# Split weights read from a second, displaced load: six vector operations in place of eight, and sums of three more attention slots on VectorE

## The chip, the cores and the metric

The kernel runs on one core of a Trainium2 chip. The metric is device time in microseconds (us) of one execution; the time of a version is the median over its runs.

## The reference

Attention with capped scores, then a mixing block ("spectral mix") on its result. B = 8 batches, H = 12 heads, S = 448 tokens, D = 64:

```python
scores = scale * np.matmul(q, k.transpose(0, 1, 3, 2))
scores = cap * np.tanh(scores / cap)
attn = np.exp(scores - max); attn = attn / sum(attn)
x = (attn @ v) laid out as [B, 448, 768]
theta = x @ w_theta
zr, zi = x * cos(theta), x * sin(theta)
u = x + w_tok_r @ zr + w_tok_i @ zi
out = u + np.maximum(u @ w_ch, 0.0)
```

The weights w_theta, w_tok_r, w_tok_i and w_ch come as 64-bit floating point numbers, the rest as float32. The kernel returns the transposed output; the host transposes it.

## The kernel before

**Work.** Attention is cut into 24 slots, three to a batch. A slot s is four heads, that is two pairs of heads (k = 2s and 2s+1); a pair's q and k are two tiles of 128 x 448 (two heads of 64 rows). Slots 0 to 3 hold attention alone. From slot LEAD = 4 on, the attention of slot s is interleaved with the mixing block of an earlier batch, a third of a batch per slot: the first third computes theta, its sine and cosine and the products (T, y, d, sc, r, f), the second mixes tokens (M), the third multiplies by w_ch (C).

**Order.** Everything stands in an order written by hand, one script of words for each kind of slot (PARTS, FRONT, OTHER at the end of the listing), and each engine runs its instructions in that order. S0 to S3 are the score matmuls (scores, L282) of a slot, t0 to t3 the tanh (L313) and e0 to e3 the exp (L326) on ScalarE (ACT); V0, W, Vr multiply by v (L376, L370), Ra and Rb sum the rows (L403); I inverts the sums and spreads them by four DMAs (L421), N multiplies (L428). The sums of slot s and its products with v, except the first ones, run in slot s+1. v loads v (L236, by the ACT queue from slot 1 on), q0, q1 load the next slot's q and k (L232, SyncE's queue, SP). The score banks in PSUM exist once, so S2 waits until t1 has read S1's scores, and v has one buffer.

**Row sums.** For s < DIRECT (direct, before 7) TensorE sums the tiles of exp themselves: 32 instructions. Else VectorE (DVE) first adds a pair's three tiles and the rest in six operations (words a0a, a0b, a1a, a1b; L346, L349, L350) and TensorE sums the result with 8.

**Weights.** A block of weights (th0 to th5: 768 words a row; tk0 to tk6: 448; ch0a to ch5b: 384) is loaded as 64-bit words and split into a high part hi and a low part lo that TensorE multiplies separately. Class Split does it: load (L135) by the queue of SP (">"), ACT ("%") or POOL ("@"); a scale on DVE ("#", L142) or on ACT ("*"); then in three parts a shift (L169), sign (L170), the AND that leaves the exponent (L153), the low word times it (L154), hi rounded (L159, or by ACT L157 for ch from 2 on), the rest (L160) and lo (L161). Which step stands in which slot is said by WEIGHTS (words w0 to w3) for th and tk and by the words that begin with ":" in slots 5 and 6 for ch. The raw words lie in large buffers, of which four (STAGES) serve th and tk; q, k and x lie in small ones.

**Queues.** DMAs issued by SP and ACT take eight counters in turn (DMAHW0 to DMAHW7 in the order below); an issue waits until the DMA before it on its counter has landed. Those of POOL have eight of their own (DMASW0 to 7).

Ahead of the branch on the size of cap the kernel loads q0, k0, th0 and th1, and TensorE runs some small matmuls (fill, L124); behind it follow q1, k1 and the scripts.

## Time and profile before

| what | value |
|---|---|
| median of 3 runs | 895.66 us (894.44 to 895.67) |
| profiled execution, its span from first to last instruction | 892.5 us |
| TensorE (PE) busy | 878.9 us, 98% |
| VectorE (DVE) busy | 658.8 us, 74% |
| ScalarE (ACT) busy | 572.9 us, 64% |
| GpSimd (POOL) busy | 92.5 us, 10% |
| chain that ended last, by engine | PE 88%, DVE 5%, ACT 2%, DMA 2%, issue 2% |
| start of slots 1, 4, 5, 6, 7 (first S0) | 22.4, 68.8, 103.0, 145.2, 184.5 us |

The profiled execution's span lies 3.2 us under the median, which includes what stands around the program. The chain of waits is followed back from the last instruction; where it lies on one engine for long, that engine sets the time there.

### The profile page before, as it was taken

To read this page: it belongs to the slowest core of one execution; us is meant where nothing else is said; L and a number is where in the kernel's file an instruction comes from. 1 tells how busy PE (TensorE), PEld (TensorE's weight loads), DVE (VectorE), ACT (ScalarE), POOL (GpSimd) and SP (SyncE) were. 2 spreads that over 40 slices of the span, in tenths; PEclk is the share of its full clock that TensorE was granted. 3 is DMA by queue.
4 is the path that set the end of the run, shared out by engine and by line. 5 is a ranking of instruction groups with operands and counts; after the bars stand their busy time and mean duration, and the time that the engine had idled before them with its cause. 6 is when DMAs were issued, how large, how long until landed. Compare 5 with 4: busy or idle time off the path is not lost.

```text
span 892.5 us, 13316 instructions
## 1 busy us (share of the span) xinstructions
PE 878.9 (98%) x4896; PEld 643.2 (72%) x4896; DVE 658.8 (74%) x1095; ACT 572.9 (64%) x652; POOL 92.5 (10%) x189
## 2 busy tenths in 40 slices
PE   8999999999999999999999999999999999999996
PEld 4325675768768678687686686776876866879995
DVE  6899779978876598675985679855987659855831
ACT  6887965658955598547975489564994459824420
POOL 0000110101300022000310012100130003100300
PEclk9999999999999999999999999999999999999998
DMA  7562464432413325122342233233151322311501
GB/s 268 191 208 73 109 172 123 151 115 72 127 50 114 94 65 152 58 88 73 107 121 68 73 108 108 80 94 114 53 145 51 104 84 80 97 42 28 139 12 55
DMA packets 50668, 90.70 MB, mean 102 GB/s; under 512 B 10913, under 2 KB 42273, under 8 KB 50593
## 3 DMA queue, kind: packets, MB, share of 16 engines
q1 hardware_dynamic: 40752, 64.62, 24.1%
q0 software_dynamic: 6384, 14.20, 5.9%
q10 hardware_dynamic: 3456, 10.95, 4.0%
q8 instruction: 40, 0.66, 0.3%
q14 instruction: 36, 0.29, 0.1%
...
## 4 chain that ended last, share of the span: by engine, by line
PE 88%; DVE 5%; ACT 2%; DMA 2%; issue 2%; SPq 1%; ACTq 0%; DVEq 0%
PE s L282 13%; PE a L376 12%; PE th L445 7%; PE th L446 7%; PE ch L445 7%; PE th L447 7%; PE ch L447 6%; PE ch L446 6%; PE mx L533 6%; PE mx L535 6%; PE mx L534 6%; PE r L403 4%; PE a L370 2%; ACT p L313 1%; DMA k<-in_qk 1%
## 5 line engine op out<-in xcount | busy, mean ns | idle before, releaser
L313 ACT ACTIVATE p<-s,qscale 128x1792 f32<-128x1792 f32 (+1 forms) x58 | 97.9, 1689 | 96.5 <-PE s L282 86.8
L506 POOL DMA_DIRECT2D t<-g_row x152 | 75.9, 506 | 536.6 <-DVE x_row L428 225.3
L533 PE MATMUL mx<-wtk_h,zh 128*128 128x448 f32 x336 | 124.4, 370 | 0.0
L535 PE MATMUL mx<-wtk_h,zl 128*128 128x448 f32 x336 | 123.4, 367 | 0.8 <-DVE zl L523 0.7
L534 PE MATMUL mx<-wtk_l,zh 128*128 128x448 f32 x336 | 122.9, 366 | 0.0
L326 ACT ACTIVATE p<-p,cap_sb 128x1792 f32<-128x1792 f32 (+1 forms) x77 | 119.9, 1558 | 2.5 <-PE a L376 1.9
L445 PE MATMUL ch<-us,wch_h 128*128 128x448 f32 x288 | 106.8, 371 | 0.4 <-DVE x L549 0.4
L445 PE MATMUL th<-xs,wth_h 128*128 128x448 f32 x288 | 106.9, 371 | 0.0
L446 PE MATMUL th<-xs,wth_h 128*128 128x448 f32 x288 | 105.5, 366 | 0.0
L447 PE MATMUL th<-xs,wth_l 128*128 128x448 f32 x288 | 105.4, 366 | 0.0
L447 PE MATMUL ch<-us,wch_l 128*128 128x448 f32 x288 | 105.3, 366 | 0.0
L446 PE MATMUL ch<-us,wch_h 128*128 128x448 f32 x288 | 105.3, 366 | 0.0
L376 PE MATMUL a<-p,v 128*64 128x448 f32 x496 | 102.6, 545 | 0.0
L376 PEld LDWEIGHTS a<-p,v 128*64 128x64 f32 x496 | 33.1, 136 | 57.1 <-issue 53.9
L533 PEld LDWEIGHTS mx<-wtk_h,zh 128*128 128x128 f32 x336 | 63.1, 188 | 10.7 <-issue 3.1
L535 PEld LDWEIGHTS mx<-wtk_h,zl 128*128 128x128 f32 x336 | 63.1, 188 | 7.6 <-DVE zl L523 2.3
L534 PEld LDWEIGHTS mx<-wtk_l,zh 128*128 128x128 f32 x336 | 63.1, 188 | 5.2
L523 DVE TENSOR_TENSOR zl<-t,zh 128x512 fp32r<-128x512 f32 x84 | 50.4, 616 | 16.5 <-ACT zh L516 15.2
L549 DVE SCALAR_TENSOR_TENSOR x<-ch,x 128x448 f32<-128x448 f32 x43 | 26.6, 621 | 48.7 <-PE ch L447 48.7
L445 PEld LDWEIGHTS ch<-us,wch_h 128*128 128x128 f32 x288 | 54.1, 188 | 10.0 <-issue 3.8
L445 PEld LDWEIGHTS th<-xs,wth_h 128*128 128x128 f32 x288 | 54.1, 188 | 9.4 <-issue 3.7
L282 PE MATMUL s<-q,k 64*128 64x448 f32 (+1 forms) x264 | 55.8, 559 | 2.5 <-DMA k<-in_qk 1.3
...
## 6 DMA issues: line engine op xcount, KB each, us to landing
v<-in_v ACTq DMA_DIRECT2D x23, 448.0 KB, 3.5
...
```

What stands on the lines that cost most here:

```text
L282: nc.tensor.matmul(out[h][:, :S], kk[rows], qq[rows], start=m == 0, stop=m == len(products) - 1)
L313: nc.scalar.activation(pp, t[:, :m, :, :S], AF.Tanh, scale=qscale)
L326: nc.scalar.activation(pp, pp, AF.Exp, scale=cap_sb)
L376: nc.tensor.matmul(acc_of["a", s, i][h * D : (h + 1) * D, :S], vt[s][:, 6 * i + 3 * h + c, :], U[s, (i, c)][:, h, :], start=first and c == ...
L445: nc.tensor.matmul(acc[:, :S], wh[:, j, ms], t[:, 0, :], start=j == 0, stop=False)
L446: nc.tensor.matmul(acc[:, :S], wh[:, j, ms], t[:, 1, :], start=False, stop=False)
L447: nc.tensor.matmul(acc[:, :S], wl[:, j, ms], t[:, 0, :], start=False, stop=j == NJ - 1)
L506: queue.dma_start(t[32 * m : 32 * m + 32, d * S : (d + 1) * S], f[32 * d : 32 * d + 32, m * S : (m + 1) * S])
L523: nc.vector.tensor_tensor(zl, tokens(b, j)[:, c0:c1], zh.bitcast(F32), op=ALU.subtract)
L533: nc.tensor.matmul(acc[:, :S], zh, wtk_h[:, c, :], start=c == 0, stop=False)
L534: nc.tensor.matmul(acc[:, :S], zh, wtk_l[:, c, :], start=False, stop=False)
L535: nc.tensor.matmul(acc[:, :S], zl, wtk_h[:, c, :], start=False, stop=c == NC2 - 1)
```

## The change

- DIRECT goes from 7 to 4: slots 4, 5 and 6 get their sums from tiles that DVE has added; the words a0a to a1b are put into the scripts of slots 4 to 6.
- Each weight block is loaded twice: once as before, and once two bytes displaced (the 16-bit view from its second element), so that a 32-bit word of the second load holds the middle bits of the 64-bit one. The split becomes six vector operations: scale, shift with AND (one instruction), sign, AND, an AND on the middle word, and one that makes lo.
- hi is no longer rounded by a cast with a subtraction behind it: it is cut by the AND. For th0 to th4 and tk0 to tk4 it is written by a DMA of the POOL queue from a working tile ("carried"), for th5, tk5, tk6 and all halves of ch by a copy on ACT. The scale of ch2b and ch3b moves to ACT.
- A th block takes two large buffers. The order of loads and splits in WEIGHTS is another: three th blocks are split in slot 0, and tk0 and tk1 are loaded behind th3.
- q1 and k1 are loaded ahead of the branch, th1 behind it; of the small buffers two move from one pool to the other.
- In slots 5 and 6 the words for ch stand in another order, and I of slot 5 earlier.

The diff, cut to its core (of the scripts, the first half of slot 5's):

```diff
-DIRECT = 7
+DIRECT = 4
...
-    w_tok = w_tok.bitcast(I32).rearrange("c p (n two) -> c p n two", two=2)
-    w_theta, w_ch = (w.bitcast(I32).rearrange("m p j (n two) -> m p j n two", two=2) for w in (w_theta, w_ch))
+    w_tok = [w_tok.bitcast(t) for t in (I32, U16)]
+    w_theta, w_ch = ([w.rearrange("m p j n -> m p (j n)").bitcast(t) for t in (I32, U16)] for w in (w_theta, w_ch))
...
-    small = Rooms(const, wk, "x", S, 2, 20)
+    small = Rooms(const, wk, "x", S, 4, 18)
...
-        def __init__(self, room, src, hi, lo, act=False):
-            self.room, self.src, self.hi, self.lo, self.act = room, src, hi, lo, act
+        def __init__(self, name, room, src, hi, lo, carried=False):
+            self.name, self.room, self.src, self.hi, self.lo, self.carried = name, room, src, hi, lo, carried
 
         def load(self, queue):
-            self.g, raw, self.t = self.room()
-            queue.dma_start(raw.bitcast(I32), self.src)
-            self.hw, self.lw = raw[..., 1], raw[..., 0]
+            self.gs, raw, self.mid, self.n = self.room()
+            queue.dma_start(raw.bitcast(I32), self.src[0])
+            queue.dma_start(self.mid.bitcast(U16)[:, : 4 * self.n - 1], self.src[1][:, 1:])
+            self.hw, self.low = raw[:, 1::2], raw[:, ::2]
+
+        def rows(self, t):
+            return t.rearrange("p (j n) -> p j n", n=P) if len(self.hi.shape) == 3 else t
...
         def part(self, stage):
+            hw, mw, lw = (self.rows(t) for t in (self.hw, self.mid[:, ::2], self.low))
             if stage == 0:
-                return self.first()
-            t, hi, lo, hw, lw = self.words, self.hi, self.lo, self.hw, self.lw
-            if stage == 1:
-                nc.vector.tensor_scalar(hw.bitcast(I32), t.bitcast(I32), -(2**23), None, op0=ALU.bitwise_and)
-                nc.vector.scalar_tensor_tensor(lw, lw.bitcast(U32), 2.0**-52, hw, op0=ALU.mult, op1=ALU.mult)
+                if self.carried:
+                    lw = self.rows(wk.tile([P, self.n], F32, tag="ps", name=f"t_{self.name}", bufs=2))
+                ti = lw.bitcast(I32)
+                nc.vector.tensor_scalar(ti, hw.bitcast(I32), 3, 0x7FFFF000, op0=ALU.logical_shift_left, op1=ALU.bitwise_and)
+                nc.vector.scalar_tensor_tensor(ti, hw.bitcast(I32), -(2**31), ti, op0=ALU.bitwise_and, op1=ALU.bitwise_or)
+                if self.carried:
+                    nc.gpsimd.dma_start(self.hi.bitcast(I32), ti)
+                nc.vector.tensor_scalar(hw.bitcast(I32), ti, -(2**23), None, op0=ALU.bitwise_and)
+            elif stage == 1:
+                nc.vector.tensor_scalar(mw.bitcast(I32), mw.bitcast(I32), 0x01FFFFFF, None, op0=ALU.bitwise_and)
             else:
-                if self.act:
-                    nc.scalar.copy(hi, t)
-                else:
-                    nc.vector.tensor_copy(hi, t)
-                nc.vector.tensor_tensor(t, t, hi.bitcast(F32), op=ALU.subtract)
-                nc.vector.tensor_tensor(lo, t, lw, op=ALU.add)
-                large.give(self.g)
-
-        def first(self):
-            t, hw = self.t, self.hw
-            if t is None:
-                t = wk.tile([P, DM], F32, tag="ps", name=f"t_{self.g.name if hasattr(self.g, 'name') else len(fills)}", bufs=2).rearrange("p (j n) -> p j n", j=NJ)
-            self.words, ti = t, t.bitcast(I32)
-            nc.vector.tensor_scalar(ti, hw.bitcast(I32), 3, None, op0=ALU.logical_shift_left)
-            nc.vector.scalar_tensor_tensor(ti, hw.bitcast(I32), -(2**31), ti, op0=ALU.bitwise_and, op1=ALU.bitwise_or)
+                if not self.carried:
+                    nc.scalar.copy(self.hi, lw)
+                nc.vector.scalar_tensor_tensor(self.lo, mw.bitcast(U32), 2.0**-36, hw, op0=ALU.mult, op1=ALU.mult)
+                for g in self.gs:
+                    large.give(g)
 
...
-            g = large.take([P, 4 * S], F32, f"{name}_raw", STAGES)
-            return g, g[:, : 2 * DM].rearrange("p (j n two) -> p j n two", j=NJ, two=2), None
+            gs = [large.take([P, 4 * S], F32, f"{name}_{part}", STAGES) for part in ("raw", "mid")]
+            return gs, gs[0][:, : 2 * DM], gs[1][:, : 2 * DM], DM
...
-            steps["th", str(m)] = Split(room_block(f"swh{m}"), w_theta[m], wth_h[:, :, ms], wth_l[:, :, ms])
+            steps["th", str(m)] = Split(f"th{m}", room_block(f"swh{m}"), [w[m] for w in w_theta], wth_h[:, :, ms], wth_l[:, :, ms], m < 5)
             for i, half in enumerate("ab"):
                 js = slice(i * NJ // 2, (i + 1) * NJ // 2)
-                steps["ch", f"{m}{half}"] = Split(room_half(f"swc{m}{half}", 1 - 2 * i), w_ch[m][:, js], wch_h[:, js, ms], wch_l[:, js, ms], m > 1)
+                src = [w[m][:, i * w.shape[2] // 2 : (i + 1) * w.shape[2] // 2] for w in w_ch]
+                steps["ch", f"{m}{half}"] = Split(f"ch{m}{half}", room_half(f"swc{m}{half}", 1 - 2 * i), src, wch_h[:, js, ms], wch_l[:, js, ms])
-            steps["tk", str(c)] = Split(room_tok(f"swk{c}"), w_tok[c], wtk_h[:, c], wtk_l[:, c])
+            steps["tk", str(c)] = Split(f"tk{c}", room_tok(f"swk{c}"), [w[c] for w in w_tok], wtk_h[:, c], wtk_l[:, c], c < 5)
...
-        (0, 0): ">th2 >tk0", (0, 1): "#th0 th0 >th3", (0, 2): "#th1 th1 >tk1", (0, 3): "#tk0 tk0 >th4",
-        (1, 0): "#th2 th2 >tk2", (1, 2): "#th3 th3 >tk3", (2, 0): "#tk1 tk1", (2, 1): "#tk2 tk2 >tk4", (2, 2): "#th4 th4 >th5", (2, 3): "",
-        (3, 0): "#tk3 tk3", (3, 1): "#tk4 tk4 >tk5", (4, 2): "#th5 th5 >tk6",
-        (4, 0): "#tk5 tk5", (4, 1): "#tk6 tk6", (4, 2): "#th5 th5 >tk6", (4, 3): "",
-        (6, 0): "#ch3a ch3a >ch4a #ch3b ch3b >ch4b", (6, 1): "#ch4a ch4a >ch5a #ch4b ch4b >ch5b", (6, 2): "#ch5a ch5a #ch5b ch5b",
+        (0, 0): ">th1", (0, 1): "#th0 th0 >th2", (0, 2): "#th1 th1 >th3", (0, 3): "#th2 th2 >tk0 >tk1",
+        (1, 0): "#th3 th3 >th4", (1, 2): "#tk0 tk0 >tk2", (1, 3): "#tk1 tk1 >tk3", (2, 0): "#th4 th4", (2, 2): "#tk2 tk2 >tk4", (2, 3): "#tk3 tk3 >tk5",
+        (3, 0): "#tk4 tk4 >tk6", (4, 2): "#tk5 tk5", (4, 0): "#tk6 tk6 >th5", (4, 1): "#th5 th5",
...
-        LEAD + 1: "S0 t0 Vr V0 Ra h0a l0a h0b l0b W h1a Rb :%ch0a cV0 cV1 :@ch0b sc2 Pa1 S1 Pb1 q0 t1 v M0a l1a r4 h1b M0b r5 l1b f4 f5 D2 e0 h2a M1a l2a m0 :#ch0a :0ch0a e1 M1b h2b l2b :1ch0a"
-        " S2 t2 M2a h3a :2ch0a :@ch1a l3a M2b h3b l3b I m1 M3a h4a l4a :#ch0b :0ch0b M3b h4b l4b :1ch0b e2 m2 S3 q1 t3 M4a h5a l5a :2ch0b :@ch1b :#ch1a :0ch1a m3 M4b"
+        LEAD + 1: "S0 t0 Vr V0 Ra h0a l0a h0b l0b W h1a Rb :%ch0a cV0 cV1 :@ch0b sc2 Pa1 S1 Pb1 q0 t1 v M0a l1a r4 h1b M0b r5 l1b I f4 f5 D2 e0 h2a M1a l2a m0 :#ch0a :ch0a :@ch1a e1 M1b h2b l2b"
+        " S2 t2 M2a h3a l3a a0a M2b h3b l3b :#ch0b :0ch0b m1 M3a h4a l4a :1ch0b :2ch0b :@ch1b M3b h4b l4b a0b e2 m2 S3 q1 t3 M4a h5a l5a :#ch1a :0ch1a m3 M4b"
...
-        for part in range(2):
-            load_raw(1, part)
...
-    for part in range(2):
-        load_raw(0, part)
-    for step in (("th", "0"), ("th", "1")):
-        steps[step].load(nc.sync)
+    for k in range(2):
+        for part in range(2):
+            load_raw(k, part)
+    steps["th", "0"].load(nc.sync)
```

The queue of SP from th2's load on, before (swh_raw, swk_raw and g_row are buffers of th and tk; in_wth is w_theta, in_wtok the token weights):

```order
L135 DMA swh_raw<-in_wth 128x1536 [waits DMAHW4_49]
L135 DMA swk_raw<-in_wtok 128x896 [waits DMAHW5_49]
L135 DMA g_row<-in_wth 128x1536 [waits DMAHW6_49,DVE_49]
L135 DMA g_row<-in_wtok 128x896 [waits DMAHW7_49,DVE_49]
L135 DMA swh_raw<-in_wth 128x1536 [waits DMAHW5_49,DMAHW0_49,DVE_49]
L232 DMA q_244<-in_qk 128x448 [waits DMAHW1_49]
L232 DMA k_246<-in_qk 128x448 [waits DMAHW2_49]
```

and with the change:

```order
L136 DMA g_row<-in_wth 128x1536 [waits DMAHW6_49,DVE_49]
L137 DMA g_row<-in_wth 128x3071 [waits DMAHW7_49]
L136 DMA swh_raw<-in_wth 128x1536 [waits DMAHW4_49,DMAHW0_49,DVE_49]
L137 DMA swh_mid<-in_wth 128x3071 [waits DMAHW5_49,DMAHW1_49]
L136 DMA g_row<-in_wtok 128x896 [waits DMAHW6_49,DMAHW2_49,DVE_49]
L137 DMA g_row<-in_wtok 128x1791 [waits DMAHW3_49]
L136 DMA g_row<-in_wtok 128x896 [waits DMAHW7_49]
L137 DMA g_row<-in_wtok 128x1791
L230 DMA q_246<-in_qk 128x448
L230 DMA k_248<-in_qk 128x448
```

The loads of th2 and th3 stand twice, tk0 and tk1 behind both, and the q and k of slot 2 behind those.

ACT at the beginning of slot 1, before:

```order
L313 ACTIVATE p_0_242<-s_0_237,qscale 128x1792 [waits PE_49]
L381 COPY x_0_258<-a_0_198 128x448
L236 DMA v_260<-in_v 128x896 [waits DMAHW7_49,DMAHW6_49,PE_49]
L326 ACTIVATE p_0_242<-p_0_242,cap_sb 128x1792 [waits Activation_49]
L313 ACTIVATE p_1_281<-s_1_274,qscale 128x1792 [waits PE_49]
```

and with the change:

```order
L311 ACTIVATE p_0_244<-s_0_239,qscale 128x1792 [waits PE_49]
L379 COPY x_0_260<-a_0_196 128x448
L234 DMA v_262<-in_v 128x896 [waits DMAHW7_49,DMAHW4_49,PE_49]
L324 ACTIVATE p_0_244<-p_0_244,cap_sb 128x1792 [waits Activation_49]
L311 ACTIVATE p_1_284<-s_1_277,qscale 128x1792 [waits PE_49]
```

The load of v waits for another counter: DMAHW4 in place of DMAHW6. Its last user ahead is tk1's first load (before: a th load).

ACT in slot 5, before (zh is the high part of z, L157 and L168 write hi of w_ch):

```order
L516 CAST zh_933<-g_row 128x384 [waits DVE_49,PE_49]
L326 ACTIVATE p_0_906<-p_0_906,cap_sb 128x1792
L516 CAST zh_933<-t_1_878 128x512 [waits DMAHW0_49,DMAHW1_49,DMASW7_49,DMAHW2_49,DMASW6_49,DMAHW3_49,DMASW5_49,DMAHW4_49,DMASW4_49,DMAHW7_49,DVE_49,PE_49]
L326 ACTIVATE p_1_970<-p_1_970,cap_sb 128x1792 [waits Activation_49]
L516 CAST zh_933<-t_1_878 128x384 [waits DVE_49,PE_49]
L313 ACTIVATE p_2_1059<-s_2_1054,qscale 128x1792 [waits DVE_49,PE_49]
```

and with the change:

```order
L514 CAST zh_929<-g_row 128x384 [waits DVE_49,PE_49]
L324 ACTIVATE p_0_915<-p_0_915,cap_sb 128x1792
L514 CAST zh_929<-t_1_887 128x512 [waits DMAHW2_49,DMAHW0_49,DMAHW3_49,DMASW7_49,DMAHW4_49,DMASW6_49,DMAHW5_49,DMASW1_49,DMAHW6_49,DMASW0_49,DMAHW7_49,DVE_49,PE_49]
L168 CAST wch_h<-g_row 128x3x128 [waits DVE_49]
L324 ACTIVATE p_1_969<-p_1_969,cap_sb 128x1792 [waits Activation_49]
L514 CAST zh_929<-t_1_887 128x384 [waits PE_49]
L311 ACTIVATE p_2_1073<-s_2_1068,qscale 128x1792 [waits PE_49]
```

The copy of ch0a's hi stands between two zh casts, ahead of e1.

## Rows read from the trace of the kernel before

**Rows 1.** The page's first part: busy us, share, instructions of each engine.
```profile
PE 878.9 (98%) x4896; PEld 643.2 (72%) x4896; DVE 658.8 (74%) x1095; ACT 572.9 (64%) x652; POOL 92.5 (10%) x189
```

**Rows 2.** Table by stage: us, then busy of PE, PEld, DVE, ACT, POOL, PEclk, DMA share, GB/s.
```profile
23.00:38.50 15.50, 15.45 (x98) 4.67 (x96) 12.49 (x20) 13.20 (x10) 0.00 (x0) 1.00 0.61 206
...
69.50:103.00 33.50, 33.50 (x182) 23.41 (x178) 30.16 (x53) 26.46 (x31) 2.28 (x4) 1.00 0.33 87
103.00:145.20 42.20, 41.94 (x223) 28.02 (x222) 31.17 (x56) 29.80 (x37) 6.14 (x12) 1.00 0.57 155
145.20:184.50 39.30, 38.02 (x205) 25.35 (x204) 37.53 (x82) 20.85 (x27) 3.84 (x7) 1.00 0.44 134
```

**Rows 3.** Chain of waits: start us, us, what; slots 1, 6 and 7.
```profile
30.87 1.73 PE s L282 x8
...
190.68 3.42 PE r L403 x32
...
227.09 0.89 PE r L403 x8
```

**Rows 4.** Timeline of ACT, slots 1 and 3: start, us, engine, operation [idle before <-releaser].
```profile
26.52 0.38 ACTq L236 DMA_DIRECT2D v<-in_v  x1
26.95 1.79 ACT L326 ACTIVATE p<-p,cap_sb 128x1792 f32<-128x1792 f32 x1 [0.65 <-PE a L376]
28.64 1.74 ACT L313 ACTIVATE p<-s,qscale 128x1792 f32<-128x1792 f32 x1
...
57.50 0.33 ACTq L236 DMA_DIRECT2D v<-in_v  x1
```

**Rows 5.** Table by stage, in the loads at the start.
```profile
4.00:6.00 2.00, 0.84 (x6) 0.63 (x8) 0.46 (x4) 0.93 (x1) 0.00 (x0) 1.00 1.03 368
6.00:8.00 2.00, 2.00 (x15) 1.03 (x12) 0.00 (x0) 1.08 (x3) 0.00 (x0) 1.00 1.02 424
```

**Rows 6.** Timeline of DVE: th0's split in slot 0, ch0a's in slot 5.
```profile
8.44 0.56 DVE L142 TENSOR_SCALAR g_row<-g_row 128x768 f32<-128x768 f32 x1 [3.95 <-DMA g_row<-in_wth]
...
9.63 0.96 DVE L170 SCALAR_TENSOR_TENSOR t_g_row<-g_row,t_g_row 128x768 int32<-128x768 int32 x1
...
123.95 0.35 DVE L142 TENSOR_SCALAR g_row<-g_row 128x384 f32<-128x384 f32 x1
...
124.73 0.56 DVE L170 SCALAR_TENSOR_TENSOR g_row<-g_row 128x384 int32<-128x384 int32 x1
```

**Rows 7.** Timeline of PE: the start, and the last matmul.
```profile
0.95 3.03 PE L124 MATMUL fill<-ones_sb 128*32 128x112 f32 x16 [0.95 <-POOL ones_sb L127]
...
7.78 1.33 PE L124 MATMUL fill<-ones_sb 128*32 128x112 f32 x12
...
11.53 0.97 PE L282 MATMUL s<-q,k 64*64 64x448 f32 x4 [1.27 <-DMA k<-in_qk]
...
884.51 0.37 PE L447 MATMUL ch<-us,wch_l 128*128 128x448 f32 x1
```

**Rows 8.** Table by stage, behind the last matmul.
```profile
887.60:889.00 1.40, 0.00 (x0) 0.00 (x0) 0.00 (x0) 0.00 (x0) 0.00 (x0) 0.54 0.02 6
```

**Rows 9.** Timeline of SP, slot 2.
```profile
54.56 0.59 SPq L135 DMA_DIRECT2D swh_raw<-in_wth  x1
```

**Rows 10.** DMA issues: queue, count, KB each, median us from issue to landing.
```profile
g_row<-in_wtok SPq DMA_DIRECT2D x4, 448.0 KB, 3.4
...
swk_raw<-in_wtok SPq DMA_DIRECT2D x3, 448.0 KB, 7.0
```

**Rows 11.** Groups of DVE: line, out<-in, count | busy us, mean ns | idle before.
```profile
L350 DVE TENSOR_TENSOR ps<-ps,g_row 64x896 f32<-64x896 f32 x34 | 36.9, 1086 | 1.2
...
L476 DVE TENSOR_SCALAR z<-z 128x448 f32<-128x448 f32 x48 | 19.0, 395 | 1.7
```

**Rows 12.** Timeline of ACT, slot 5.
```profile
124.11 0.51 ACT L516 CAST zh<-t 128x384 fp32r<-128x384 f32 x1
```

**Rows 13.** Timeline of POOL, slot 4.
```profile
98.02 2.28 POOL L506 DMA_DIRECT2D g_row<-f  x4 [97.13 <-DVE f L495]
```

15 lines of the change are left out of this document (7 added, 8 removed).

## The prediction

> **What bounds the kernel now.** I read the page's first part first: PE is busy 878.9 of 892.5 us and no other engine over 74% [rows 1]. So the end moves only by what changes PE's own work, or by what opens a gap on PE. Next the table by stage [rows 2]: in slot 1 (23.0 to 38.5) PE works 15.45 of 15.50 us, ACT 13.20 and DVE 12.49; in slots 4, 5 and 6 DVE works 30.16 of 33.5, 31.17 of 42.2 and 37.53 of 39.3 us. An instruction more on DVE costs nothing in the first slots and something in slot 6, where DVE is as full as PE. The chain of waits gives the prices of PE's own pieces [rows 3], and PE's timeline the one transfer that holds it near the start, the second pair's k [rows 7].
>
> The profiled span is 892.5 us. The runs have a median of 895.66, so 3.2 us lie around it, and I add the same to the new span. A difference within 0.2% (1.8 us: 893.9 to 897.5) counts as no change.
>
> **Second pair first.** S1 of slot 0 waits for k1 and starts at 11.53 behind a gap of 1.27 us [rows 7]. With q1 and k1 ahead of the branch this gap goes: -1.3 us, and slot 1 begins near 21.1. That gain survives only if the next item doesn't swallow it.
>
> **The doubled loads.** This is the term I hold largest. In slot 1 ACT issues the load of v between the copy of x and e0 (26.52, then e0 at 26.95 and t1 at 28.64 [rows 4]). It stands in ACT's order, so all behind it stands too. DMAs share eight counters in turn, and an issue waits until the previous DMA of its counter has landed. Before, the counter's last user was an early th load; now it is the first load of tk1 (order above: DMAHW4 for DMAHW6). That load is issued only when th2 has been split, and lies behind nearly all that is moved at the start. Bytes ahead, from the shapes in the diff: eight q and k loads 1.84 MB, v 0.46, th0 to th3 twice 6.29, tk0 twice and tk1's first 1.38: 9.96 MB, and three copies of hi 1.18. The DMA engines are full at 368 to 424 GB/s [rows 5]; at 396 from about 3.2 us. th2's second load is 7.0 MB into the list: 3.2 + 17.7 = 20.9 us. Its split is four operations of 0.56 and two of 0.96 [rows 6], 4.2 us: 25.1. By then th3 and two copies still keep the queues full till about 26.9, so tk1 continues the list: 11.14 MB / 0.396 = 28.1, so 31.3, and with the notice of landing about 32.0 (at 424: 29.5, at 368: 33.5).
>
> ACT comes to that issue at about 25.3 (26.52 less the 1.27) and stands 6 to 7 us. After it: the issue 0.38, e0 1.79, t1 1.74 [rows 4], together 3.9, and S2 needs t1 since the score banks exist once. So S2 of slot 1 starts at about 36.0 where it started at 30.87 [rows 3]: **+5.2 us**, the gain of the second pair already inside. PE has 0.05 us of room in a slot and ACT some 2, so later slots do not win this back. Bounds: -1.3 (it lands before 25.3) and +6.7 (368 GB/s). No row shows a load from a displaced address; the nearest is the straight one, and I take that price. Its other end, displaced loads half as fast, adds 3.6 MB / 0.396 = 9 us.
>
> By the Trainium skill (DMA: Bandwidth & Descriptors, "How a descriptor splits into AXI transactions") a descriptor that doesn't start on a 256-byte address is fetched from the boundary below it; a displaced 6142-byte row would take 25 transactions in place of 24, an estimate of 4% or 0.4 us on those 9, and the sum would be 0.4 higher. No row here shows it, and I leave it out of the sum.
>
> **A gap has its echo.** PE would stand from about 29.6 to 36. After the last matmul at 884.51 the granted clock stood at 1.00 for some 3 us and then fell to 0.54 [rows 7, 8], half of 2.4 GHz. A gap of 6 us is longer, one of 1.27 in slot 0 was not. The nearest price of a cold start: the first sixteen fills took 3.03 us, twelve later ones of the same shape 1.33 [rows 7], so sixteen warm would be 1.77: **+1.3** (between 0 and 2).
>
> **The later v loads.** In slot 2 the same wait is on tk2's first load, by my count half a microsecond ahead: nothing, but it can fail. In slot 3 it is on tk5's first load, which SP issues behind four issues of reciprocals, on the old times where a th load was issued at 54.56 [rows 9], so at about 54.9. With the 3.4 us that a tok load takes to landing [rows 10] that is 58.3, against 57.50 when ACT reached it [rows 4]: 0.8, and tk4's second load just ahead makes it **+1.2**. Ends: 0, and with the 7.0 us of the slower tok loads [rows 10] +4.4.
>
> **Sums of slots 4 to 6.** A slot's sums as 32 instructions take 3.42 us, as 8 from a pre-added tile 0.89 [rows 3]. Three slots change (each is summed in the slot after it): 3 x 2.53 = **-7.6 us** of PE's own work, the only real saving on the path.
>
> **What DVE pays for it.** Six adds of 1.09 [rows 11] in each of three slots are +19.4 us on DVE. The split gives back: two operations of 0.96 for th5 (1.9), two of 0.63 for tk5 and tk6 (2.5), and per half of ch a subtraction and addition of 0.56 less one more AND of 0.35, with the cast as well on the four halves where DVE had it (4 x 1.3 + 8 x 0.75), and two scales of 0.35 that go to ACT [rows 6]: about 16.3 in all. That takes a shift with an AND in one instruction at the price of one operation, as the two-operation form shows (395 ns for 448 columns [rows 11]). Its other end, twice the price, would cost 16 blocks' extra passes, of which some 5 us fall into slots 4 to 6. So DVE has about 3 us more in slots 4 to 6, where it had 3.3, 11.0 and 1.8 free [rows 2].
>
> Worse than the sum is the order. hi is now written by ACT for th5, tk5, tk6 and every half of ch. In slot 5 the copy of ch0a stands between two zh casts and in front of e1 (order above) and waits for DVE's shift and sign. zh at 124.11 [rows 12] would come after e1 (1.80) and the copy (0.5) and whatever DVE, busy with its first adds, is late: 3 to 5 us later, and the matmuls of M2b take it soon after; I put PE's wait at 2.6, an estimate. In slot 4 the copy of th5 sits between t2 and t3 and holds ACT by up to 2 us. I book **+4.3** as given back of the 7.6, so slots 4 to 7 come to -3.3; ends -6.7 (only 0.9 lost) and +2 (DVE becomes the bound in slot 6).
>
> **Sum.** +5.2 + 1.3 + 1.2 - 7.6 + 4.3 = **+4.4**: span 896.9, time **900.1 us**.
>
> **Rivals.** (1) *The wait never bites.* The point that decides is whether tk1's first load lands by about 26 us. For it: DMA share in slot 1 before is only 0.61 [rows 2], so the queues do drain, and if th2 is split early tk1 can overtake. Against it: 11 MB can't move by 26 at any rate that a row shows. Then there is no gap and no cold start, the second pair's 1.3 is kept, slot 3's 1.2 goes half away: 895.7 - 1.3 - 3.3 + 0.6 = 891.7; with all of the sums 887.4. (2) *The two sides cancel.* The wait ends near 29.5, so the gap on PE is short enough for the clock to stand: +2.7 + 0 + 0.6, and DVE's fewer operations keep up in slots 5 and 6: -6.7. Middle 893 to 897, say 896. (3) *Copies held up.* The ten copies of hi are issued by POOL while DVE is busy; ps has two buffers, so th2's shift waits for th0's copy to land. Four POOL issues took 2.28 us in slot 4 with DVE busy nine tenths of the time [rows 2, 13], which speaks against. If they are held till DVE pauses, th2's split and so tk1's load come a split later, 4.2 us: 904.3; with displaced loads at half speed as well 909. The Trainium skill (SBUF — State Buffer, "SBUF: two separate sides") has such a rule: an operation of DVE in a two-port mode shuts GpSimd out from writing descriptors for its DMAs. The 0.57 us an issue in that row doesn't show it. (4) *The split isn't shorter*: if the shift with AND costs two passes, slots 4 to 6 give back all 7.6: 903.4.
>
> **How the numbers follow.** Forecast 0.50, with its own range 897 to 905 (0.46 slower, 0.04 same). Rival 1 0.22 (0.20 faster, 0.02 same). Rival 2 0.12 (0.02 faster, 0.09 same, 0.01 slower). Rival 3 0.12 and rival 4 0.04, both slower. Together faster 0.22, same 0.15, slower 0.63. The range of 8 in 10 takes most of rival 1 and the near half of rival 3: 889.5 to 906.
>
> **What would show it.** Right: ACT's issue of v in slot 1 ends idle of 4 us or more with a tok load named as releaser; PE idle from about 29.6 to 36, and slower matmuls behind it; sums of 0.89 in slots 5 to 7; slot 4 starting some 7.7 us later than 68.8, slot 7 some 7 later than 184.5, slot 8 some 4 late. Wrong: ACT issuing v before 27, slot 4 starting earlier than 68.8, or PE gaps in slots 5 and 6 as small as before, which would leave the full 7.6.

## The result, and the profile after

The change makes the kernel slower: 906.79 us (905.18 to 909.49, 4 runs) against 895.24 (4 runs), ratio 1.0133, 95% interval 1.0114 to 1.0152. The forecast was 900.1 with a range of 889.5 to 906.0: the direction held, the size did not. The profiled execution took 909.49 us, 2.7 above the median, and its span is 907.6; between span and time lie about 1.9 us in these runs, not the 3.2 that the prediction took from the median of before.

The page of the changed kernel, first part, and the chain of waits by engine:

```profile
PE 879.9 (97%) x4824; PEld 643.0 (71%) x4824; DVE 646.9 (71%) x1069; ACT 577.1 (64%) x661; POOL 105.7 (12%) x210
PE 82%; DVE 6%; DMA 5%; ACT 3%; issue 3%; SPq 2%; POOL 0%; ACTq 0%; DVEq 0%; POOLq 0%
```

PE is busy 1.0 us longer than before [rows 1], although 7.6 us of its sums are gone: half-speed matmuls have taken their place. DMA's share of the chain has grown from 2 to 5%. The table by stage shows the stretch, its length, the busy time of PE, PEld, DVE, ACT and POOL, then PE's granted clock (PEclk), the DMA share and GB/s. Slots 1, 4, 5 and 6:

```profile
22.00:50.80 28.80, 18.24 (x100) 5.34 (x98) 14.07 (x24) 13.71 (x11) 3.10 (x4) 0.76 0.81 287
86.00:120.30 34.30, 34.30 (x188) 23.94 (x186) 28.31 (x49) 28.10 (x34) 1.98 (x4) 1.00 0.34 105
120.30:166.90 46.60, 41.59 (x199) 27.15 (x198) 36.16 (x60) 30.89 (x39) 8.56 (x17) 1.00 0.67 178
166.90:205.40 38.50, 36.55 (x181) 24.40 (x181) 35.27 (x73) 23.35 (x32) 7.69 (x14) 1.00 0.63 218
```

Slot 1 has grown from 15.5 [rows 2] to 28.8 us, at a mean granted clock of 0.76. Slot 5 has grown from 42.2 to 46.6, slot 6 shrunk by 0.8. So there are two losses, far apart. The first is the one of the forecast. ACT in slot 1 (start, us, operation [idle before]):

```profile
25.48 0.53 ACT L379 COPY x<-a 128x448 f32<-128x448 f32 x1
37.22 0.38 ACTq L234 DMA_DIRECT2D v<-in_v  x1
37.65 1.79 ACT L324 ACTIVATE p<-p,cap_sb 128x1792 f32<-128x1792 f32 x1 [11.64 <-issue]
```

The issue of v, at 26.52 before [rows 4], stands until 37.22. SP had issued tk1's first load only at 28.80, and PE waits for t1:

```profile
28.80 0.67 SPq L136 DMA_DIRECT2D g_row<-in_wtok  x1
```

```profile
27.98 2.60 PE L401 MATMUL r<-p,ones_sb 128*32 128x448 f32 x24
41.13 2.61 PE L280 MATMUL s<-q,k 64*128 64x448 f32 x6 [10.56 <-ACT p L311]
```

Behind the gap PE runs at half its clock (a granted 0.50) for 5.6 us or a little more, as the table by stage shows:

```profile
41.20:46.80 5.60, 5.60 (x20) 1.62 (x24) 0.59 (x1) 4.22 (x4) 0.00 (x0) 0.50 0.56 217
47.20:52.00 4.80, 4.80 (x26) 1.76 (x24) 4.59 (x10) 2.97 (x3) 0.57 (x1) 1.00 0.57 138
```

The same view of the stretches before it shows why the load came late: the DMA engines are full nearly without a break, at 331 to 390 GB/s. The first row takes the whole stretch together, from the first weight loads to the issue of v.

```profile
3.00:37.20 34.20, 26.38 (x159) 11.37 (x156) 17.00 (x28) 16.25 (x12) 3.70 (x4) 0.94 0.98 358
11.00:23.00 12.00, 11.70 (x75) 5.44 (x76) 6.62 (x10) 10.90 (x8) 2.04 (x2) 1.00 1.01 390
23.00:33.00 10.00, 7.58 (x54) 1.91 (x50) 7.65 (x12) 2.18 (x2) 0.83 (x1) 1.00 0.95 331
33.00:43.00 10.00, 1.87 (x6) 1.06 (x8) 1.08 (x2) 5.35 (x4) 0.83 (x1) 0.52 1.02 378
```

In the list of DMA issues (KB each, median us to landing) the displaced loads stand beside the straight ones:

```profile
swh_raw<-in_wth SPq DMA_DIRECT2D x4, 768.0 KB, 7.4
...
g_row<-in_wth SPq DMA_DIRECT2D x3, 767.8 KB, 8.0
swh_mid<-in_wth SPq DMA_DIRECT2D x3, 767.8 KB, 11.0
...
g_row<-in_wth SPq DMA_DIRECT2D x2, 768.0 KB, 8.1
```

These times don't tell whether a displaced load (767.8 KB) is slower in itself than a straight one (768.0 KB), since each displaced load is issued right behind its straight one and stands behind it in the queue. The single packets of the trace tell it. Up to 45 us 640 straight packets of 6144 bytes took a median of 235 ns, and 633 displaced ones of 6142 bytes also 235. So a displaced load is just another load in a full queue. By the rule of the Trainium skill (DMA: Bandwidth & Descriptors, "How a descriptor splits into AXI transactions") a row that starts two bytes behind a 256-byte boundary and ends on one takes as many transactions as the straight row, 24, if the straight rows start on a boundary; the prediction had counted 25. The trace agrees with 24, by the two medians of 235 ns.

Slot 4 starts 17.2 us late in this execution. From there to slot 8 the kernel takes 153.3 us where it took 152.2. The sums' 7.6 us are saved (each takes 0.89 as in [rows 3]), so 8.8 us are given back. Of these, 5.4 us stand as longer waits of PE (7.0 us idle against 1.5); the rest is in matmuls that take longer. Behind slot 8 the kernel then takes 3.3 us less than before, 1.1 of it up to the last matmul and 2.2 behind that. So the span is 15.1 us longer and not 18.4.

This execution is the slowest of the change's four. Six runs below (e3, e6, e7, e8, e11, e13) do the same work in slots 0 to 3, and in their profiled executions that part is quicker: v is issued at 34.2 to 35.2 and not at 37.2, S2 of slot 1 starts at 38.1 to 39.1 and not at 41.1, and slot 4 at 82.5 to 84.4 and not at 86.0.

### The profile page after: what moved, and what is told of

Its sections match the earlier page's. It is cut to its first block, busy times and chain, and to the rows that moved or that the text cites. A ratio compares the mean times of both kernels' runs of the same rounds, so it can differ in the third digit from the quotient of the medians.

```text
span 907.6 us, 13228 instructions
## 1 busy us (share of the span) xinstructions
PE 879.9 (97%) x4824; PEld 643.0 (71%) x4824; DVE 646.9 (71%) x1069; ACT 577.1 (64%) x661; POOL 105.7 (12%) x210
## 4 chain that ended last, share of the span: by engine, by line
PE 82%; DVE 6%; DMA 5%; ACT 3%; issue 3%; SPq 2%; POOL 0%; ACTq 0%; DVEq 0%; POOLq 0%
PE s L280 11%; PE a L374 10%; PE mx L531 7%; PE mx L533 7%; PE mx L532 7%; PE th L443 6%; PE ch L443 6%; PE th L444 6%; PE th L445 6%; PE ch L445 6%; PE ch L444 6%; PE r L401 3%; DMA g_row<-in_wth 2%; PE a L368 2%; SPq L504 1%
## 5 line engine op out<-in xcount | busy, mean ns | idle before, releaser
L280 PE MATMUL s<-q,k 64*128 64x448 f32 (+1 forms) x232 | 51.5, 588 | 13.4 <-ACT p L311 12.5
L514 ACT CAST zh<-t 128x512 fp32r<-128x512 f32 x84 | 45.3, 562 | 20.9 <-PE mx L532 19.1
```

The costliest lines, as they stand in the source:

```text
L280: nc.tensor.matmul(out[h][:, :S], kk[rows], qq[rows], start=m == 0, stop=m == len(products) - 1)
```

## The experiments

The times below are medians, and the ratios are against the kernel before. "Slot 1", "slot 4" are the starts of the first score matmul, read from PE's timeline of each run; "S2" is that of slot 1; the last column is the time from slot 4's start to slot 8's. These four columns are of one profiled execution each.

| run | us | ratio, 95% | slot 1 | S2 | slot 4 | slots 4 to 8 |
|---|---|---|---|---|---|---|
| before | 895.2 to 895.8 | | 22.3 | 30.8 | 68.8 | 152.2 |
| the change | 906.79 | 1.0114 to 1.0152 | 22.0 | 41.1 | 86.0 | 153.3 |
| e1_v_pool | 901.04 | 1.0045 to 1.0078 | 20.1 | 28.6 | 78.2 | 152.7 |
| e2_one_load | 895.47 | 0.9988 to 1.0007 | 20.1 | 28.6 | 68.8 | 153.6 |
| e3_direct7 | 910.04 | 1.0152 to 1.0186 | 20.1 | 38.5 | 82.9 | 153.9 |
| e4_sums_only | 902.64 | 1.0065 to 1.0099 | 22.2 | 30.7 | 68.7 | 160.3 |
| e5_paced | 899.71 | 1.0033 to 1.0067 | 20.0 | 28.5 | 76.1 | 153.2 |
| e6_invert_back | 904.83 | 1.0095 to 1.0128 | 22.1 | 39.1 | 83.4 | 150.0 |
| e7_copy_later | 906.70 | 1.0107 to 1.0146 | 21.8 | 39.0 | 84.4 | 153.1 |
| e8_ch_one_load | 903.35 | 1.0077 to 1.0111 | 21.9 | 38.1 | 82.5 | 150.2 |
| e9_pair_early | 894.15 | 0.9975 to 0.9994 | 22.2 | 30.7 | 68.7 | 151.8 |
| e10_hybrid | 893.20 | 0.9969 to 0.9988 | 22.0 | 30.5 | 68.5 | 152.2 |
| e11_d7_invert_back | 907.80 | 1.0128 to 1.0161 | 22.0 | 38.6 | 83.3 | 151.3 |
| e12_hybrid_d7 | 894.38 | 0.9979 to 0.9998 | 20.1 | 28.6 | 66.6 | 153.8 |
| e13_direct5 | 905.24 | 1.0093 to 1.0127 | 22.2 | 38.5 | 82.9 | 151.7 |
| e14_hybrid_d5 | 893.67 | 0.9964 to 0.9985 | 22.0 | 30.5 | 68.5 | 153.2 |
| e15_hybrid_d5_copy | 893.12 | 0.9956 to 0.9979 | 22.1 | 30.6 | 68.6 | 151.7 |

Slot 1 starts at 20.1 in some profiled executions and at 22.0 in others of the same opening; the last section says why. It is chance, so the early slots are compared with that in mind.

Two more things bear on the columns. In five executions PE also ran at half its clock for some us inside slots 5 and 6, each time in or behind a wait of 1.8 to 4.7 us: e2 (140.9 to 144.3), e4 (160.8 to 167.6), e5 (147.7 to 151.1), e7 (155.4 to 158.8) and e12 (123.3 to 126.7). Up to half of such a stretch, 1.7 us and in e4 3.4, is lost time in their last column. And the kernels differ behind slot 8 as well: from there to the last matmul the executions take 662.6 to 665.1 us, and behind the last matmul 5.4 to 7.6. So a difference of a microsecond between two medians is not always one of slots 4 to 8.

### The early slots: counter, order or bytes

**e1_v_pool.** 

> The changed kernel, with v of slots 1 to 3 loaded by POOL's queue, whose DMAs have counters of their own; nothing else differs, and as many bytes move. Theory A (ACT stands at v's issue because its shared counter's last user, tk1's first load, lands at 37): ACT's e0 of slot 1 starts near 26 and not at 37.65, S2 of slot 1 near 31 and not at 41.13, the granted clock stays at 1.00, slot 4 starts near 69 to 71 and not at 86; time 891 to 896. Theory B (the DMA engines are full anyway, so v itself lands late and PE only waits for it at another place): V0 of slot 1 waits until about 37, slot 4 starts at 78 or later; time above 900. What slots 5 and 6 lose stays by both.

```diff
-        (nc.scalar if s else nc.sync).dma_start(vt[s], v[s // NP2, s % NP2])
+        (nc.sync if s == 0 else nc.gpsimd if s < LEAD else nc.scalar).dma_start(vt[s], v[s // NP2, s % NP2])
```

Each theory holds in part. S2 of slot 1 is on time (28.6) and ACT waits no more, as theory A had it. But the gap has moved to the matmuls that need v, the clock falls behind it all the same (half from 34.5 to 44.7), and the time is theory B's. PE, and under it POOL:

```profile
39.07 1.77 PE L361 MATMUL a<-p,v 64*64 64x448 f32 x8 [7.86 <-DMA v<-in_v]
```

```profile
29.83 0.84 POOL L162 DMA_DIRECT2D wth_h<-t_th  x1 [7.24 <-issue]
30.66 0.57 POOL L234 DMA_DIRECT2D v<-in_v  x1
```

v was issued at 30.66, behind a copy of hi that POOL could not issue earlier, and landed 8.3 us later (before: 3.5 us in the median of all v loads). The counter was the door at which the kernel waited; behind it stood a full queue. The time is 5.8 us (0.6%) under the change's.

**e2_one_load** leaves out the second load of th0 to th4 and tk0 to tk4, so lo of these blocks is made from other bits. 

> The changed kernel without the second load of the ten blocks whose hi is carried (th0 to th4, tk0 to tk4): their middle word is taken from the low word instead, so lo of these blocks is not the right one; instructions on all engines stay as many and as large. It takes 6 MB of 100 away, all ahead of slot 4. Theory A and the volume: the queues drain in slot 0, v's counter belongs to a load that landed long before, S2 of slot 1 at 30 to 31, no half clock, slot 4 at 67.5 to 69; time 890 to 894, not clearly under e1. If the copies of hi by POOL (theory: descriptors held up while DVE works) were the cause, th2's split would still end after 27 and S2 of slot 1 come after 35; time above 898.

```diff
-            queue.dma_start(self.mid.bitcast(U16)[:, : 4 * self.n - 1], self.src[1][:, 1:])
+            if not self.carried:
+                queue.dma_start(self.mid.bitcast(U16)[:, : 4 * self.n - 1], self.src[1][:, 1:])
+            else:
+                self.mid = raw
```

All copies of hi, all operations and the adds stay, and the early loss is gone: S2 at 28.6, slot 4 at 68.8. What is still lost stands in slot 3, where v's issue waits on ACT for tk5, which comes twice here too. ACT in that slot:

```profile
57.27 1.79 ACT L327 ACTIVATE p<-p,cap_sb 128x1792 f32<-128x1792 f32 x1 [2.01 <-DMA swk_raw<-in_wtok]
```

So the copies by POOL and DVE's work are not the cause. Leaving loads out also shifts which counter v's issue waits on, so e2 alone doesn't part the bytes from the counter. Taken with e1, where v waits for no shared counter and still lands late, it is the bytes ahead in the queue and not the counter alone. The time, 895.47, is 1.5 us above the expected 890 to 894: slots 4 to 8 came out at 153.6, with 3.4 us of half clock among them.

**e5_paced** tells whether order can replace fewer bytes. 

> The changed kernel with as many bytes, in another order: v of slots 1 to 3 is issued by SP ahead of that slot's weight loads, and th3, tk0 and tk1 are loaded behind v of slot 1 instead of ahead of it (the other loads shift along, the splits keep their size). Theory F (first come, first served: the DMA engines are full from 3 to 43 us, and what attention needs stands behind weights that nobody needs before slot 4): no PE wait over 1 us and no half clock in slots 1 to 3, slot 4 starts at 66.5 to 69, time 890 to 894. Theory V (the doubled volume itself is too much for slots 0 to 3): PE still waits for v, q or k or DVE for raw words, slot 4 starts at 74 or later, time above 898.

```diff
-        (0, 0): ">th1", (0, 1): "#th0 th0 >th2", (0, 2): "#th1 th1 >th3", (0, 3): "#th2 th2 >tk0 >tk1",
-        (1, 0): "#th3 th3 >th4", (1, 2): "#tk0 tk0 >tk2", (1, 3): "#tk1 tk1 >tk3", (2, 0): "#th4 th4",
+        (0, 0): ">th1", (0, 1): "#th0 th0 >th2", (0, 2): "#th1 th1", (0, 3): "#th2 th2",
+        (1, 0): ">th3 >tk0 >tk1", (1, 2): "#th3 th3 >th4", (1, 3): "#tk0 tk0 >tk2", (2, 0): "#tk1 tk1 >tk3", (2, 1): "#th4 th4",
...
-        (nc.scalar if s else nc.sync).dma_start(vt[s], v[s // NP2, s % NP2])
+        (nc.scalar if s >= LEAD else nc.sync).dma_start(vt[s], v[s // NP2, s % NP2])
```

(the rest of the loads shift along, which is not shown.)

The outcome is theory V's, in slot 4's start and in the time, though theory F holds for slot 1 (S2 at 28.5). What was put off is still to be moved, and slot 2's v meets it; the table by stage of that stretch stands under PE's row:

```profile
54.03 1.77 PE L361 MATMUL a<-p,v 64*64 64x448 f32 x8 [7.36 <-DMA v<-in_v]
```

```profile
43.00:53.00 10.00, 3.67 (x28) 1.00 (x24) 7.03 (x13) 6.01 (x5) 1.62 (x2) 0.78 1.03 392
```

The engines are now full from 3 to 63 us (a share of 1.01, 363 GB/s). Two things make up the wait of 7.4 us: SP came to slot 2's v only at 45.10, behind its weight loads, and the load took 8.8 us to land.

### Slots 4 to 7: the sums and what they cost

**e3_direct7.** 

> The changed kernel with DIRECT back at 7: slots 4 to 6 are summed by TensorE's 32 instructions, and the adds on DVE go. Theory C (slots 5 and 6 lose time since the adds fill DVE, and all behind stands in line): PE's extra 7.6 us is met by as many us of waits less, the time is 905 to 908, no change. Theory D (they lose it since the doubled ch loads hold up the carries and ACT's copies of hi stand in its order; the adds are hidden): the sums' 7.6 us come on top, 911 to 915.

```diff
-DIRECT = 4
+DIRECT = 7
```

From slot 4 to slot 8 it takes 153.9 us against 153.3. That is theory C's mechanism: 7.6 us of sums more come out as only 0.6 us more, with PE 4.6 us longer busy and 4.0 us less idle. The time, 910.04, lies between the two forecasts. By the medians the adds are worth 3.2 us, more than these slots show; 1.0 of it lies between slot 8 and the last matmul, and where the rest lies is open.

**e4_sums_only.** 

> The kernel before with DIRECT at 4 and the adds put into slots 5 and 6 at the places of the changed kernel; the split, the loads and the order of the blocks are those of before. Theory C: 19.4 us of adds on a DVE that gets nothing back: slots 5 and 6 lose what the sums save or more, 895 to 901. Theory D: DVE has 11 us free in slot 5 and 3 in slot 4, only slot 6 gives back: slot 7 starts 0 to 5 us earlier than 184.5, time 888 to 892.

```diff
-DIRECT = 7
+DIRECT = 4
-        " S2 t2 M2a h3a :2ch0a :@ch1a l3a M2b
+        " S2 t2 M2a h3a :2ch0a :@ch1a l3a a0a M2b
```

(and a0b to a1b likewise). Theory C again, and stronger than expected, with a time above both ranges: slots 4 to 8 take 160.3, 8.1 us more than before with 7.6 us less of sums on PE. DVE is busy 37.56 of 39 us here. ACT's tanh waits 7.06 us for DVE's split of ch, and PE for that tanh:

```profile
145.00:184.00 39.00, 33.04 (x158) 20.98 (x157) 37.56 (x75) 17.15 (x23) 4.39 (x8) 0.91 0.38 117
```

```profile
160.10 1.75 ACT L313 ACTIVATE p<-s,qscale 128x1792 f32<-128x1792 f32 x1 [7.06 <-DVE wch_l L161]
161.91 3.66 PE L282 MATMUL s<-q,k 64*64 64x448 f32 x12 [4.74 <-ACT p L313]
```

In that wait the clock falls to half, for 6.8 us, which adds to the loss. So the adds on a DVE with the old split cost more than they save. In the change the same adds stand in slots that take 7 us less (153.3); that this is owed to the shorter split, and not to another part of the change, is argued and not shown.

**e6_invert_back.** 

> The changed kernel with the word I of slot 5 (three operations of DVE, four DMAs of SP) back at its old place behind the second group's l3b; nothing else. Theory P (the earlier I puts 2.6 us of issues ahead of the twelve carries on SP, so zh of M4a comes late): the wait of 2.2 us at M4a goes, slot 6 starts 2 to 5 us earlier against slot 4 than in the changed kernel (there 80.9 us after it), time 902 to 905. By the rival (adds on DVE, or doubled ch loads) it stays within 0.5 us at slot 7.

```diff
-M0b r5 l1b I f4 f5 D2 e0
+M0b r5 l1b f4 f5 D2 e0
...
-a0a M2b h3b l3b :#ch0b
+a0a M2b h3b l3b I :#ch0b
```

Theory P: 150.0, 3.3 us regained, and the time as expected. In the changed kernel SP issues the four DMAs of I (bc) ahead of the twelve carries (g_row<-f, the copies that hand a part of f from one third of a batch to the next), and zh of M4a, on ACT, waits 7.0 us. The row names a load of q as its releaser; SP issues that one right behind the carries, whose last issue ends at 152.65:

```profile
140.05 2.58 SPq L419 DMA_DIRECT2D bc<-ri  x4
142.74 9.91 SPq L504 DMA_DIRECT2D g_row<-f  x12
```

```profile
144.43 0.56 ACT L168 CAST wch_h<-g_row 128x384 fp32r<-128x384 f32 x1 [3.32 <-DVE g_row L160]
...
156.65 0.62 ACT L514 CAST zh<-g_row 128x512 fp32r<-128x512 f32 x1 [7.00 <-DMA q<-in_qk]
```

PE's waits in that slot, two of them for it:

```profile
133.17 0.47 PE L533 MATMUL mx<-wtk_h,zl 128*128 128x448 f32 x1 [1.44 <-DVE zl L521]
147.13 0.47 PE L531 MATMUL mx<-wtk_h,zh 128*128 128x448 f32 x1 [1.20 <-ACT zh L514]
157.32 0.47 PE L531 MATMUL mx<-wtk_h,zh 128*128 128x448 f32 x1 [2.21 <-ACT zh L514]
```

With I put back SP has the carries first, and zh starts 4.2 us behind their end as it did 4.0 behind it in the change. PE's third wait is gone, the second 0.26:

```profile
137.55 8.80 SPq L504 DMA_DIRECT2D g_row<-f  x12
149.01 2.42 SPq L419 DMA_DIRECT2D bc<-ri  x4
```

```profile
150.57 0.62 ACT L514 CAST zh<-g_row 128x512 fp32r<-128x512 f32 x1 [4.88 <-DVE swc0b_raw L160]
```

**e8_ch_one_load** leaves out the second load of the ch halves; lo of w_ch is made from other bits. 

> The changed kernel without the second load of the twelve ch halves: the middle word is taken from the high word instead, so lo of w_ch is not the right one; all engines' instructions stay as many and as large. Theory D (the doubled ch loads hold up carries and casts in slots 5 and 6): slot 7 starts 3 to 6 us earlier against slot 4 than in the changed kernel (119.4 us after it), time 901 to 904. If the adds and the order set the pace there: under 1 us of difference.

```diff
+            if self.name[:2] != "ch":
                 queue.dma_start(self.mid.bitcast(U16)[:, : 4 * self.n - 1], self.src[1][:, 1:])
```

(the AND on the middle word reads the high word). Theory D by its lower end: 150.2, 3.1 us regained, and the time as expected. SP is through the carries in 8.8 us here, not in 9.9, and zh starts 1.8 us behind their end. Since both e6 and e8 bring zh of M4a forward, their gains need not add up; the two together were not tried.

**e7_copy_later.** 

> The changed kernel with ACT's copy of ch0a's hi moved behind e1 and the next zh casts; DVE keeps its order but for nothing. Theory Q (the copy, waiting for DVE, holds e1 and zh of M2b): ACT's idle of 3.3 us in front of that copy and PE's 1.2 us at M2b go, slot 6 starts 1 to 3 us earlier against slot 4, time 904 to 906. By the rival that DVE's work or the carries set the pace of slot 5, the wait turns up later and slot 7 starts where it did.

```diff
-:#ch0a :ch0a :@ch1a e1 M1b h2b l2b
+:#ch0a :0ch0a :1ch0a e1 M1b h2b l2b
...
-S2 t2 M2a h3a l3a a0a
+S2 t2 M2a h3a :2ch0a :@ch1a l3a a0a
```

The rival: 153.1. The wait at M2b goes, but zh of M4a now starts 4.6 us behind the carries' end and PE waits 4.60 us there. From that wait on the clock is at half for 3.4 us, so up to 1.7 us of what the move may have saved are lost there.

**e11_d7_invert_back** and **e13_direct5** take the adds away again with I put back, all of them and those of slot 4. 

> The changed kernel with I of slot 5 back at its old place and DIRECT at 7: against the run with I put back alone it shows what the adds on DVE give back when the carries are on time. If DVE hides the adds, slots 4 to 8 take the 7.6 us of PE's sums longer than there: 157 to 158 against 150.0, time 911 to 913. If the adds give back most of them: 151 to 153, time 905 to 907.

> The changed kernel with I of slot 5 put back and DIRECT at 5: slot 4 is summed by TensorE's 32 instructions again, slots 5 and 6 from DVE's adds. Theory H (the last three adds of slot 4 stand on DVE in front of the rotation, the flip and the carries at the head of slot 5, so all of that slot's matmuls come about 2 us late): the 2.5 us of sums come back and the same time of waits goes, from slot 4 to slot 8 149.5 to 150.5 us, as with DIRECT at 4 (150.0), and S2 of slot 5 starts level with DIRECT at 7. If slot 4's adds are hidden: 152.5.

```diff
-DIRECT = 4
+DIRECT = 7
```

(5 in e13, in both with the diff of e6). From slot 4 to 8 it takes 151.3 without adds, 151.7 with those of slots 5 and 6, 150.0 with all. By these single executions the adds of slots 5 and 6 save 5.1 us of PE's sums and cost 5.4, and those of slot 4 save 2.5 and keep 1.6. The medians divide it the other way: 907.80 without adds, 905.24 with those of slots 5 and 6, 904.83 with all. By them the adds of slots 5 and 6 are worth 2.6 us, and slot 4's can't be told from nothing. Part of the gap lies behind slot 8, where e11 takes 2.0 us longer to the last matmul than e13. So all adds together keep some 3 of the 7.6 us, and how that divides over the slots stays open.

Theory H's total fell between its two forecasts (151.7), though its mechanism is in the trace and S2 of slot 5 starts level in e11 and e13, as it had it. With slot 4's adds, DVE does three of them at the head of slot 5, in front of the rotation (L485), which stood 1.2 us behind the slot's start before and stands 4.1 behind it in the changed kernel:

```profile
120.90 1.09 DVE L344 TENSOR_TENSOR ps<-p 128x896 f32<-128x896 f32 x1
122.09 1.09 DVE L347 TENSOR_TENSOR ps<-ps,p 128x896 f32<-128x896 f32 x1
123.21 1.09 DVE L348 TENSOR_TENSOR ps<-ps,p 64x896 f32<-64x896 f32 x1
124.33 1.09 DVE L485 TENSOR_TENSOR z<-z,x 128x896 f32<-128x896 f32 x1
```

Of the 2.7 us that slot 4's adds have saved at its sums in e6, 2.0 are lost again by S2 of slot 5; without those adds (DIRECT of 5 or 7) none is lost there. Behind that S2, up to slot 6's start, e13 takes 2.0 us longer than before and e6 1.7, and in slot 6 e6 gains 0.6 more. Why the later stretch loses more where slot 4's adds are missing stays open.

### Parts that stand alone, and together

**e9_pair_early.** 

> The kernel before with q1 and k1 loaded ahead of the branch, together with the first pair, and nothing else. By the gap at 11.53 it should save 1.3 us; the early part of the runs without doubled loads says 2.2: slot 1 starts near 20.1 instead of 22.30, slot 4 near 66.6, 892.9 to 893.9. By the rival (th0 lands later and DVE's splits hold up the next slots) the gain is gone by slot 4: 895.

```diff
-    for part in range(2):
-        load_raw(0, part)
+    for k in range(2):
+        for part in range(2):
+            load_raw(k, part)
```

894.15, 1.4 us less, interval 0.9975 to 0.9994: the gain of 1.3 is there in the medians. The profiled execution can't show it, since its clock came late (slot 1 at 22.2). Against before's 22.3 the executions of the pair-early kernels whose clock came early start slot 1 at 20.0 to 20.1.

**e10_hybrid, e12_hybrid_d7, e14_hybrid_d5, e15_hybrid_d5_copy.** 

> The parts of the change that the runs so far leave standing, together: second pair early, th and tk loaded once and split in eight operations in the order of before, ch loaded twice and split in six, sums of slots 4 to 6 from DVE's adds, I of slot 5 back at its old place. If the doubled th and tk loads were what the early slots lost, slot 4 starts near 66.6; from there to slot 8 the changed kernel with I put back took 150.0 us against 152.2 before, with DVE 4 us lighter in slot 4: 150 to 153. Time 890.5 to 893.5, under before. By the rival (the copies of ch's hi and the adds cost more than they save once DVE has the old th5, tk5 and tk6 again) 155 and more, time 895 to 899.

> The hybrid with DIRECT at 7, so no adds on DVE in slots 4 to 6: second pair early, th and tk as before, ch loaded twice and split in six. Slots 4 to 8: 150.5 to 152.2 (before 152.2, of which some 1.5 us are waits for DVE that a shorter split takes away), time 891.5 to 893.5; against the hybrid it tells whether the sums are worth their adds in the best surroundings.

> The hybrid (second pair early; th and tk loaded once, eight operations, order of before; ch loaded twice, six operations; I of slot 5 at its old place) with DIRECT at 5. With DVE 4 us fuller in slot 4 than in the changed kernel the adds of slot 4 should cost more than they save: slots 4 to 8 in 150.5 to 152 against 152.2 with DIRECT at 4, time 891.5 to 893. By the rival (the loss at the head of slot 5 has another cause, as the run with DIRECT at 7 lost 3 us there as well) 153 and more, 894.

> The same with ACT's copy of ch0a's hi moved behind e1 and the next zh casts. In the changed kernel that move gave nothing, since M4a then waited for the carries behind I. With I back, theory Q says the 1.2 us at M2b go and stay gone: 1 to 1.5 us under the run beside it, 890 to 892. By the rival that the carries or DVE set the pace of slot 5 even so: the same within 0.5 us.

```diff
-            steps["th", str(m)] = Split(f"th{m}", room_block(f"swh{m}"), [w[m] for w in w_theta], wth_h[:, :, ms], wth_l[:, :, ms], m < 5)
+            steps["th", str(m)] = Split8(room_block(f"swh{m}"), w_theta[0][m].rearrange("p (j n two) -> p j n two", j=NJ, two=2), wth_h[:, :, ms], wth_l[:, :, ms])
...
-    steps["th", "0"].load(nc.sync)
+    for step in (("th", "0"), ("th", "1")):
+        steps[step].load(nc.sync)
```

(Split8 is the split of before; tk likewise, with the order of before, and I as in e6.) All four are faster than before, and e15 is the fastest of the study: 893.12 us, ratio 0.9967 (0.9956 to 0.9979). Slot 4 starts where it did before, or 2.2 us sooner in e12, whose clock came early. e10 met its range. e12 missed its own by 0.9 us (894.38; slots 4 to 8 took 153.8, with 3.4 us of half clock among them). In e14 the rival's figures came (153.2 and 893.67), so the adds of slot 4 keep 0.9 us by the traces (e10 took 152.2); by the medians, 893.20 and 893.67 with intervals that overlap, that can't be told from nothing. In e15 the copy of ch0a's hi is moved back in ACT's order. Its trace is 1.4 us shorter than e14's, but the medians differ by only 0.55 us with intervals that overlap, the time misses the expected 890 to 892, and a new wait of 0.90 us stands at M4a. So that this move is worth anything is not shown.

## Why the prediction was wrong

**Right.** The place and the mechanism of the first loss: v's issue on ACT, the landing of tk1's first load, t1, S2, and a half clock behind it. The prices of sums (0.89), of the adds (1.09) and of shift with AND as one operation (0.56 for 768 words in the trace after): rival 4 is out. The copy of ch0a's hi and M2b's wait (1.2 us where 2.6 was booked).

**The doubled loads: +5.2 forecast, +10.3 measured at S2 here, +7.3 to +8.3 in the six other executions.** The step that failed is the landing of tk1's first load, put at 32.0; v's issue shows it at 34.2 to 35.2 in the six and at 37.2 here. The list of bytes was right, the rate was not. From 3.0 to 37.2 us the engines moved 358 GB/s, and 352 to 365 in the other executions, where the prediction took 396 from two stretches of 2 us [rows 5]. At 358 its 11.14 MB take 31.1 us and land at 34.3; with its 0.7 us for the notice, which no row shows, that is 35.0, where the six executions lie. The further 2.2 us are this execution's: DVE came to th2's split at 23.67, behind th1's, whose second load had taken 12.3 us to land. The split was done by 27.9 and not 25.1, and tk1, issued at 28.80, took 8.4 us. The slowest row that the prediction shows, 368 GB/s, set its upper end for this term (+6.7), and the whole stretch was slower than that row. That the clock came late at the start here adds nothing to this: e3, whose clock came early, has S2 at 38.5, and e11 and e13, whose clock came late, at 38.6 and 38.5. The prediction's 25 transactions for a displaced row are a miscount, as said above; they stood outside its sum.

**The echo: +1.3 forecast, 2.7 measured in slot 1, and a second one.** The half clock lasted 5.6 us or a little more behind the restart, longer than the sixteen fills; S2 to the next slot's start grew by 2.7 us (1.5 to 2.7 over the seven executions with this opening). A second gap in slot 3, where v waits for tk5 as forecast (2.0 us where 1.2 was booked), brought another 1.5. Slot 2, booked at nothing, lost 0.8. Only one restart had a price.

**Slots 4 to 7: -3.3 forecast, +1.2 measured.** The step that failed is the +4.3 given back, which was 8.8. The sum compared DVE's busy time with the slot's length and found 11 us free in slot 5. They are not free where they are needed: in that slot DVE, ACT's zh, the carries and PE hand work on in turn, and three adds ahead of the rotation delay S2 of slot 5 by 2.0 us (e6 against e13). Two parts of the change stand in no term of the sum, without a reason: I's move, and the doubled ch loads. Taking either out gives back 3 us (3.3 in e6, 3.1 in e8). And of what the sums save, the adds leave some 3 of 7.6 us by the medians of e3 and of e11 against e6.

**The total.** From slot 4 to the end the change comes out 2.1 us under before, near the -3.3 of the forecast, but by luck: the 3.3 us gained behind slot 8 were no part of it. So nearly all of the miss in the time sits in slots 0 to 3, +17.2 us here and +13.7 to +15.6 in the six others against the +7.7 forecast.

**Rivals.** Rival 1 failed at its own point: nothing moves 11 MB by 26 us. Rival 2 fell as well, since the wait ended at 34 to 37 and the clock did fall; its own terms add up to 892.3 and not to 893 to 897. Rival 3 gave the size (904.3 to 909, where its two terms together make 913.3) by another cause: e2 keeps every copy of hi and loses the early wait, so the copies were not it. They were held up all the same: POOL issued the second at 22.08 though its words were ready at 19.2. In the trace after, these are the copies and the spread of their landing:

```profile
L162 POOL DMA_DIRECT2D wth_h<-t_th x5: 829/867/1169, 12.3 to 57.6; - x5
...
DMA to landing us min/median/max: 2.7/6.6/9.5
```

The first, issued at 12.29, took 9.5 us to land, and 0.3 us behind that the second went out, at 22.08. The third (27.11) and the fourth (34.73) also went out some 0.3 us behind the landing of the one before. In e2, without the second loads, each went out as soon as DVE had made its words, the second at 18.36. The second of the changed kernel, and under it that of e2:

```profile
22.08 0.87 POOL L162 DMA_DIRECT2D wth_h<-t_th  x1 [8.62 <-issue]
```

```profile
18.36 0.85 POOL L165 DMA_DIRECT2D wth_h<-t_th  x1 [4.83 <-DVE t_th L163]
```

So the copies were held up where the queues were full. That each waits for the one before it is argued from these times, not tried. The rule of the Trainium skill that I named beside the rival (SBUF — State Buffer, "SBUF: two separate sides") would end such a wait with DVE's operation; DVE stood idle from 19.8 to 22.0, so it isn't what these rows show.
